# Two of V's 32 key blocks in one group of each layer: from 128 partitions to partitions 0 to 63, in eight-row transfers on ACT's queue

## The chip, the cores and the metric

The kernel runs on one core of one Trainium2 chip. The metric is the time of one execution on the device in microseconds; the figure used is the median of three runs. TensorE, VectorE, ScalarE, GpSimd and SyncE are called PE, DVE, ACT, POOL and SP, as in the profile. The core's transfers run on 16 DMA engines; a transfer is issued by an instruction on SP or on ACT.

## The reference, cut to what matters

Two layers, each a one-token attention step over a cached K and V and then an MLP, in float32:

```python
def _A_ref(x, k_cache, v_cache, wq, wo):
    q = (x @ wq).reshape(B, Sq, H, Dh)            # 32 heads of 128
    scores = einsum("bhqd,bhkd->bhqk", q, k_cache) * Dh ** -0.5
    p = softmax(scores)                           # over 4096 keys
    o = einsum("bhqk,bhkd->bhqd", p, v_cache)
    return o.reshape(B, Sq, H * Dh) @ wo
def _B_ref(x, w1, b1, w2, b2):
    return gelu(layernorm(x) @ w1 + b1) @ w2 + b2
...
x = x + _A_ref(_layernorm(x), k_cache, v_cache, wq, wo)
x = x + _B_ref(_layernorm(x), w1, b1, w2, b2)
```

The last two lines run twice with the same weights and the same K and V, so K and V (67 MB each) are read nearly whole in both layers.

## The kernel before, in words

The 32 heads are taken in eight groups of four (`G`, `J`). Layer 0 runs the groups 0 to 7, layer 1 runs them 7 to 0; `n` counts the groups inside a layer. The host has laid K, V and the weights out so that a group's K is one array of 128 rows by 16384 floats, its V another one. Eight chunks (`C`) of 2048 columns (`NC`) make up such an array; a chunk of V holds four blocks of 128 keys for the four heads (`U` = 512 columns each), so a group's V has 32 blocks. A key's row lies on the partition that is its number modulo 128.

For one group the program does this. `stream` (L356) issues one SP transfer of 128 rows of 64 KB for K through `load` (L83, the issue itself at L85). `scores` (L211) multiplies each chunk by the query, into the PSUM tile `pS`. `softmax` (L216) takes the maximum on DVE, the exponential on ACT (L223), and four PE transposes (L225), so that the weights lie with keys on partitions (`pt`, written by DVE at L227). `stream` issues V in the same way, and `values` (L238) multiplies each chunk by its weights, four matmuls of 512 columns per chunk into `pO` (L241). `scaled_out` (L244) turns the result, `head_out` (L264) multiplies it by the group's Wo (L269), and `queries` (L201) makes the next group's query (L203 to L208). The next group's Wo and Wq are one SP transfer.

All loaded data lives in one large tile, `arena`, which holds three group arrays of 64 KB a partition in turn and some space behind them (`HELD`, `PAIR`). A transfer is issued when its place is free, that is when PE or DVE has read what lay there. SP's order is the order of the calls of `load`. There are 78 transfers from memory on SP, all of 128 rows, and none on another engine. Every transfer also takes one of eight completion counters in turn and waits until the transfer that had it before has landed.

The last group of a layer and the MLP load in smaller pieces. In layer 0 the MLP's matmuls L295 (w1) and L343 (w2) follow the last attention pieces, and the first transfers of layer 1 are issued as these matmuls free their places. The kernel ends with L343 of layer 1, an addition on DVE (L527) and a store of 4 rows (L528). `idle` (L367, the matmul at L368) issues matmuls whose result nobody reads; six stand behind the first group's scores in layer 0.

PE's instructions are themselves fetched from memory while the program runs. The profile lists these fetches as queues of the kind "instruction" (q8 and q14), beside q1, which carries SP's transfers.

Of the kernel before, what the change touches and what calls it, by code (L numbers as in the profile page):

```python
# [17 lines left out]
P = 128  # L18
# [3 lines left out]
G = 8  # L22
J = 4
C = 8
# [3 lines left out]
U = 512  # L28
KEPT = 6

NC = 4 * U
BLOCK = 8 * NC
# [3 lines left out]
HELD = SPARE + 2 * NC  # L36
# [14 lines left out]
FILL = 3  # L51
LAST = ((0, 4), (4, 6), (6, 7))
LAST_IDLE = {3: 1, 5: 1, 6: 1}
WHOLE, HALVES = ((0, 8),), ((0, 4), (4, 8))
VAR_AT = 1


@with_exitstack
def decode_layers(ctx: ExitStack, tc: tile.TileContext, k, v, w, w1, w2, out):
    nc = tc.nc  # L60
# [20 lines left out]
    arena = const.tile([P, ARENA], F32, name="arena")  # L81

    def load(at, src):  # L83
        t = arena[:, at : at + src.shape[-1]]
        tc.keep_in_program_order(nc.sync.dma_start(t, src))  # L85
        return t
# [41 lines left out]
    row, _ = wq_at(0)  # L128
# [3 lines left out]
    ident = ctile("ident", P)  # L132
# [7 lines left out]
    pS, pO, pB = (psum.tile([P, 512], F32, name=n) for n in ("pS", "pO", "pB"))  # L140
# [75 lines left out]
    def softmax(sc, nsc, p):  # L216
        nc.vector.tensor_reduce(mx[:, 0:1], pS, axis=AX.X, op=ALU.max)  # L217
        mt, m, bias = small("mt", 32), small("m"), small("lr", 32)
        nc.vector.transpose(mt, mx)
        nc.vector.tensor_reduce(m, mt[:, :C], axis=AX.X, op=ALU.max)  # L220
        nc.vector.tensor_scalar(mb[:, :C], m.to_broadcast([P, C]), nsc, None, op0=ALU.mult)
        nc.vector.transpose(bias, mb)  # L222
        nc.scalar.activation(p, pS, AF.Exp, bias=bias[:, 0:1], scale=sc, accum_out=mx[:, 0:1])  # L223
        for b in range(4):
            nc.tensor.transpose(pT[:, b].rearrange("p j r -> p (j r)"), p[:, P * b : P * (b + 1)], ident)  # L225
        pt = work.tile([P, J, C, 4], F32, name="pt")
        nc.vector.tensor_copy(pt, pT[:, :, :, :C].rearrange("p b j c -> p j c b"))  # L227
        lt, l, lr, rl = small("mt", 32), small("l"), small("lr", 32), small("rl")
        nc.vector.transpose(lt, mx)  # L229
        nc.vector.tensor_reduce(l, lt[:, :C], axis=AX.X, op=ALU.add)  # L230
        nc.vector.tensor_copy(lt, l.to_broadcast([P, 32]))
        nc.vector.transpose(lr, lt)
        nc.vector.reciprocal(rl, lr[:, 0:1])
        return pt, rl

    def by_head(vt):
        return vt.rearrange("p b (j d) -> p j b d", j=J)

    def values(i, pt, vt, c, of=C):
        for j in range(J):  # L240
            nc.tensor.matmul(pO[32 * j : 32 * j + 4, :], pt[:, j, c, :], by_head(vt)[:, j],  # L241
                             start=(i == 0), stop=(i == of - 1))

    def scaled_out(rl, ot):  # L244
        nc.vector.transpose(ot[:, :512], pO)  # L245
        diag = ot.rearrange("p (b q) -> p b q", q=129)[:, :, :P]
        diag = diag.rearrange("p b (d q) -> p d b q", q=32)[:, :, :, 0]
        o, on = small("o", 4), small("on", 4)
        nc.vector.tensor_reduce(o, diag, axis=AX.X, op=ALU.add)
        nc.vector.tensor_scalar(on, o, rl, None, op0=ALU.mult)  # L250
        return on
# [104 lines left out]
    def stream(what, g, pieces, base):  # L356

        for a, b in pieces:
            t = load(base + NC * a, part(k if what == "k" else v, g, a, b))
            for c in range(a, b):  # L360
                here[what, g, c] = chunk(t, c - a)
                yield c, here[what, g, c]
# [7 lines left out]
    for layer in range(2):  # L370
        order = list(range(G)) if layer == 0 else list(range(G))[::-1]
# [21 lines left out]
        for n, g in enumerate(order):  # L393
# [6 lines left out]
            if layer == 1 and n == 0:  # L400
                tiles = [(c, here["k", g, c]) for c in range(C)]
            elif layer == 1 and n == 1:
                tiles = [(c, here["k", g, c]) for c in range(2)]
                tiles += list(stream("k", g, ((2, 4), (4, 8)), -2 * NC))
                n_kept = STAY + U * KEPT
                load(V1_HOME[6] + n_kept % NC, v[g][:, n_kept:BLOCK])
                for u in range(STAY, n_kept - U, U):
                    nc.scalar.copy(v_next(u), pK[(u - STAY) // U])
                for c in range(STAY // NC, C):
                    here["v", g, c] = chunk(arena[:, V1_HOME[c] : V1_HOME[c] + NC])  # L410
            elif layer == 1 and n == 2:
                tiles = [(c, here["k", g, c]) for c in range(6)]
                tiles += list(stream("k", g, ((6, 8),), 2 * BLOCK - 6 * NC))
            else:
                tiles = stream("k", g, HALVES if first or final else WHOLE, k_home)
            for c, t in tiles:
                scores(z, c, t)
            if first or final:
                for _ in range(FILL if final or layer == 1 else 2 * FILL):
                    idle(t, pO)  # L420
            p, ot = free_now(layer, n)
            if layer == 1 and first:
                z = queries(n + 1, xc_l, wq_next, pO)
                nc.scalar.copy(v_next(STAY + U * KEPT - U), pB)
            pt, rl = softmax(sc, nsc, p)
            if final:
                nc.scalar.activation(small("m"), rl, AF.Gelu_apprx_tanh)

            if layer == 1 and n == 0:
                for c in range(C):  # L430
                    values(c, pt, here["v", g, c], c)
            elif layer == 1 and n == 1:
                for c in range(C):
                    values(c, pt, here["v", g, c], c)

                for pieces, base in ((((0, 4),), K2_HOME), (((4, 6),), SPARE - 4 * NC)):
                    for _ in stream("k", order[2], pieces, base):
                        pass
            elif final:
                last_v = chunk(arena[:, v_home + BLOCK - NC : v_home + BLOCK])  # L440
                for _ in range(FILL - 1):
                    idle(t, pS)
                for c, t in stream("v", g, LAST, v_home):
                    values(c, pt, t, c, C - 1)
                    if c == C - 2:
                        others = scaled_out(rl, ot)
                    for _ in range(LAST_IDLE.get(c, 0)):
                        idle(t, pS)
                for a in (BLOCK - NC, BLOCK - NC // 2):
                    load(v_home + a, v[g][:, a : a + NC // 2])  # L450
                for c in range(C):
                    here["v", g, c] = chunk(arena[:, v_home + NC * c : v_home + NC * (c + 1)])
            else:
                for c, t in stream("v", g, WHOLE, v_home):
                    for i in range(KEPT - 1):
                        if layer == 0 and n == G - 2 and c == (STAY + U * i) // NC:
                            nc.scalar.copy(pK[i], t[:, STAY // U % J + i - J * (c - STAY // NC), :])
                    values(c, pt, t, c)

            if layer == 1 and n == 0:  # L460
                wo_t = chunk(arena[:, PAIR : PAIR + NC])
# [113 lines left out]
```

## Time and profile before

| what | value |
|---|---|
| median of 3 runs | 677.62 us (677.26 to 677.77) |
| the profiled execution's own time | 677.63 us |
| its span, first to last instruction | 675.9 us |
| busy share of PE, DVE, ACT | 60%, 17%, 4% |
| mean granted TensorE clock | 0.806 |
| mean DMA rate over the span | 422 GB/s |

The span leaves out 1.7 us that lie around it. The profile names DMA queues, and gives each packet's time and size, but not which of the 16 engines carried it. A share of 16 engines' time in a stretch is the sum of the times of the packets that start in it, so a short stretch with long packets can show more than 100%.

### The profile page before, as it was taken

How to read it: one execution, taken by the hardware profiler on the slowest of the kernel's cores; microseconds unless marked ns; L12 is line 12 of the kernel's file. 1: busy time of each engine (PE TensorE's matmuls, PEld its weight loads, DVE VectorE, ACT ScalarE, POOL GpSimd, SP SyncE). 2: the span in 40 equal slices, each digit the busy share in tenths (PEclk: the TensorE clock that was granted, in tenths of full speed). 3: DMA queues.
4: the chain of work that ended last, by engine and by line, in shares of the span. 5: the costliest groups of instructions: out<-in, count | busy, mean ns of one | idle time of the engine just before them, and what ended most of it. 6: DMA issues, size and time to landing. Idle time of an engine off the chain costs nothing.

```text
span 675.9 us, 6740 instructions
## 1 busy us (share of the span) xinstructions
PE 408.1 (60%) x3008; PEld 109.8 (16%) x3008; DVE 115.2 (17%) x369; ACT 27.4 (4%) x57; POOL 5.0 (1%) x24
## 2 busy tenths in 40 slices
PE   2745664565534854467597986674466545755596
PEld 1111111111111111111124321111111111111123
DVE  3002110120021201212022322120121111200212
ACT  0010000000000000001011200000000000000010
POOL 1000000000000000000000000000000000000000
PEclk9779776797678865878899998976797767976899
DMA  9999999999999999999999999999999999999995
GB/s 374 435 434 434 435 435 434 413 457 432 428 427 422 444 434 432 434 432 417 433 410 353 427 418 462 407 447 435 426 432 431 432 434 409 461 432 411 426 414 234
DMA packets 11268, 285.34 MB, mean 422 GB/s; under 512 B 1252, under 2 KB 1256, under 8 KB 3688
## 3 DMA queue, kind: packets, MB, share of 16 engines
q1 hardware_dynamic: 11240, 284.92, 98.6%
q8 instruction: 23, 0.38, 0.2%
q14 instruction: 5, 0.04, 0.0%
HBM read 284.92 MB, written 0.00 MB: 422 GB/s over the span
## 4 chain that ended last, share of the span: by engine, by line
PE 40%; DMA 39%; another core or an unknown queue 14%; DVE 4%; ACT 1%; issue 1%; ACTq 0%; SPq 0%; DVEq 0%
DMA arena<-in_v 35%; PE pO L241 19%; PE pS L213 12%; DMA arena<-in_w 4%; PE pB L269 4%; PE pO L207 1%; PE pO L225 1%; ACT arena L223 1%; PE pS L368 1%; DVE arena L245 1%; DVE smalls L217 1%; PE pO L368 0%; PE pO L343 0%; DVE arena L205 0%
## 5 line engine op out<-in xcount | busy, mean ns | idle before, releaser
L213 PE MATMUL pS<-arena,smalls 128*8 128x512 f32 x1024 | 148.3, 732 | 112.5 <-DMA arena<-in_k 111.6
L241 PE MATMUL pO<-arena,pt 128*4 128x512 f32 x1008 | 139.9, 700 | 79.1 <-DMA arena<-in_v 78.6
L269 PE MATMUL pB<-arena,smalls 128*1 128x512 f32 x112 | 52.8, 616 | 21.9 <-DVE smalls L250 15.9
L213 PEld LDWEIGHTS pS<-arena,smalls 128*8 128x8 f32 x1024 | 30.1, 103 | 214.9 <-issue 190.9
L241 PEld LDWEIGHTS pO<-arena,pt 128*4 128x4 f32 x1008 | 28.4, 95 | 178.0 <-issue 175.2
L217 DVE TENSOR_REDUCE smalls<-pS 128x1 f32<-128x512 f32 x16 | 11.1, 692 | 253.1 <-PE pS L213 253.1
L245 DVE STREAM_TRANSPOSE arena<-pO 128x512 f32<-128x512 f32 x16 | 11.5, 717 | 217.1 <-PE pO L241 217.1
L223 ACT ACTIVATE arena<-pS,smalls 128x512 f32<-128x512 f32 x16 | 12.4, 778 | 536.2 <-DVE smalls L222 536.2
L205 DVE SCALAR_TENSOR_TENSOR arena<-arena,smalls 128x512 f32<-128x512 f32 x45 | 33.8, 752 | 1.6
L225 PE MATMUL pO<-ident,arena 128*128 128x128 f32 x64 | 13.2, 341 | 33.8 <-ACT arena L223 33.5
L269 PEld LDWEIGHTS pB<-arena,smalls 128*1 128x1 f32 x112 | 8.6, 85 | 65.9 <-issue 38.2
L207 PE MATMUL pO<-smalls,arena 128*128 128x1 f32 x120 | 16.6, 259 | 3.3 <-DVE arena L205 3.3
L207 PEld LDWEIGHTS pO<-smalls,arena 128*128 128x128 f32 x120 | 15.3, 200 | 15.5 <-DVE arena L205 13.8
L225 PEld LDWEIGHTS pO<-ident,arena 128*128 128x128 f32 x64 | 8.5, 169 | 47.7 <-ACT arena L223 46.5
L368 PE MATMUL pO<-arena,ident 128*8 128x512 f32 (+1 forms) x38 | 15.9, 547 | 0.0
L368 PE MATMUL pS<-arena,ident 128*8 128x512 f32 (+1 forms) x34 | 14.0, 517 | 0.5 <-DVE pt L307 0.5
L203 DVE TENSOR_SCALAR arena<-arena,smalls 128x512 f32<-128x512 f32 x15 | 7.2, 480 | 4.7 <-DMA arena<-in_w 4.7
L343 PE MATMUL pO<-arena,smalls 128*1 128x128 f32 x176 | 5.9, 272 | 3.3 <-DMA arena<-in_w 2.2
L208 DVE COPY smalls<-pO 128x4 f32<-128x4 f32 x15 | 2.5, 165 | 26.5 <-PE pO L207 26.5
L169 PE MATMUL pO<-smalls 128*32 128x1 f32 x64 | 2.0, 184 | 7.4 <-DVE smalls L163 6.3
L229 DVE STREAM_TRANSPOSE smalls<-smalls 128x32 f32<-128x32 f32 x16 | 3.4, 211 | 17.5 <-ACT arena L223 17.5
L295 PE MATMUL pS<-arena,smalls 128*2 128x128 f32 (+1 forms) x160 | 4.9, 259 | 1.9 <-DMA arena<-in_w 1.9
(92 smaller groups left out, 101.2 us busy)
## 6 DMA issues: line engine op xcount, KB each, us to landing
arena<-in_k SPq DMA_DIRECT2D x8, 4096.0 KB, 26.0
arena<-in_w SPq DMA_DIRECT2D x13, 2048.0 KB, 33.2
arena<-in_v SPq DMA_DIRECT2D x2, 4096.0 KB, 38.4
arena<-in_k SPq DMA_DIRECT2D x3, 2048.0 KB, 15.9
arena<-in_v SPq DMA_DIRECT2D x2, 2048.0 KB, 41.6
arena<-in_w SPq DMA_DIRECT2D x4, 1024.0 KB, 16.3
arena<-in_w SPq DMA_DIRECT2D x6, 512.0 KB, 13.3
arena<-in_v SPq DMA_DIRECT2D x2, 1024.0 KB, 43.2
```

Of the source, the lines that this page charges most:

```text
L203: pin(nc.vector.tensor_scalar(t, wt[:, 0, :], xc[:, 0:1], None, op0=ALU.mult))
L205: nc.vector.scalar_tensor_tensor(t, wt[:, c, :], xc[:, c : c + 1], t, op0=ALU.mult, op1=ALU.add)
L207: nc.tensor.matmul(at[:, j : j + 1], t[:, P * j : P * (j + 1)], one, start=True, stop=True)
L213: nc.tensor.matmul(pS[32 * j : 32 * j + C, :], z[:, j, C - 1 - c : 2 * C - 1 - c], kt[:, j, :], start=(c == 0), stop=(c == C - 1))
L217: nc.vector.tensor_reduce(mx[:, 0:1], pS, axis=AX.X, op=ALU.max)
L223: nc.scalar.activation(p, pS, AF.Exp, bias=bias[:, 0:1], scale=sc, accum_out=mx[:, 0:1])
L225: nc.tensor.transpose(pT[:, b].rearrange("p j r -> p (j r)"), p[:, P * b : P * (b + 1)], ident)
L241: nc.tensor.matmul(pO[32 * j : 32 * j + 4, :], pt[:, j, c, :], by_head(vt)[:, j], start=(i == 0), stop=(i == of - 1))
L245: nc.vector.transpose(ot[:, :512], pO)
L269: nc.tensor.matmul(pB[0:1, :], on[:, d : d + 1], wt[:, d, :], start=n == 0 and d == 0, stop=n == G - 2 and d == 3)
L343: pin(nc.tensor.matmul(pM[32 * j : 32 * j + 1, :], g[:, c - b0 : c - b0 + 1], w2_t[c][:, P * j : P * (j + 1)], start=(c == 0), stop=(c == ...
L368: pin(nc.tensor.matmul(at[:C, :n], ident[:, :C], t[:, 0, :n], start=True, stop=True))
```

## The change

In one group of each layer (`MOVED_OF`: group n = 4 in layer 0, n = 5 in layer 1) the last two blocks of V's 32, 1024 columns, are no longer part of the 128-row V transfer, which is 15360 columns there. The host copies the half of these blocks that lay on partitions 64 to 127 into unused columns behind rows 0 to 63 of the array, so that each of the rows 0 to 63 holds 2048 contiguous columns, 8 KB: its own half and that of row 64 higher. `load_moved` brings them in with eight transfers of eight rows each (row numbers first, first + 4, ... first + 28), issued on ACT's queue: three, three and two of them in the three groups ahead of the one that uses them. The same bytes are read in all.

In that group `second_half` makes two more PE transposes and a DVE copy, to bring the weights of keys 64 to 127 to partitions 0 to 63, and the last chunk's four matmuls of 512 columns become twelve of 256 columns (`values_in_halves`). Also, the six idle matmuls of the first group in layer 0 go.

```diff
+LOWER, MOVED = P // 2, 2
+MOVED_OF = 4, 5
+MOVED_ROWS = {1: (0, 3), 2: (3, 6), 3: (6, 8)}, {2: (0, 3), 3: (3, 6), 4: (6, 8)}
+MOVED_AT = 3 * BLOCK, 2 * BLOCK + 2 * NC
+HALF_AT = HELD + 2 * NC + U + 4 * 129, 2 * BLOCK + 3 * NC
...
+    def load_moved(layer, g, parts):
+        t = arena[:LOWER, MOVED_AT[layer] : MOVED_AT[layer] + 2 * MOVED * U]
+        for q in range(*parts):
+            first = q % 4 + 32 * (q // 4)
+            rows = slice(first, first + 29, 4)
+            nc.scalar.dma_start(t[rows], v[g][rows, BLOCK - MOVED * U : BLOCK + MOVED * U])
+        return t.rearrange("p (h b j d) -> h p j b d", h=2, b=MOVED, j=J)
+
+    def second_half(layer, p):
+        for i in range(MOVED):
+            b = 4 - MOVED + i
+            nc.tensor.transpose(pO[:LOWER, P * i : P * (i + 1)], p[:, P * b + LOWER : P * (b + 1)], ident)
+        t = arena[:LOWER, HALF_AT[layer] : HALF_AT[layer] + J * MOVED].rearrange("p (j b) -> p j b", j=J)
+        nc.vector.tensor_copy(t, pO[:LOWER, : P * MOVED].rearrange("p (b j r) -> p j b r", b=MOVED, j=J)[:, :, :, C - 1])
+        return t
+
+    def values_in_halves(pt, pt_half, vt, moved):
+        b = 4 - MOVED
+        for j in range(J):
+            at = pO[32 * j : 32 * j + 4]
+            nc.tensor.matmul(at[:MOVED, : P * MOVED], pt_half[:, j], moved[1][:, j], start=False, stop=False)
+            nc.tensor.matmul(at[:, P * b :], pt[:LOWER, j, C - 1, :], moved[0][:, j], start=False, stop=False)
+            nc.tensor.matmul(at[:, : P * b], pt[:, j, C - 1, :], by_head(vt)[:, j, :b], start=False, stop=True)
...
+            halved = n == MOVED_OF[layer]
+            if n in MOVED_ROWS[layer]:
+                moved = load_moved(layer, order[MOVED_OF[layer]], MOVED_ROWS[layer][n])
             for c, t in tiles:
                 scores(z, c, t)
             if first or final:
-                for _ in range(FILL if final or layer == 1 else 2 * FILL):
+                for _ in range(FILL if final or layer == 1 else 0):
                     idle(t, pO)
...
             pt, rl = softmax(sc, nsc, p)
+            if halved:
+                pt_half = second_half(layer, p)
...
-                for c, t in stream("v", g, WHOLE, v_home):
+                if halved:
+                    t = load(v_home, v[g][:, : BLOCK - MOVED * U])
...
-                    values(c, pt, t, c)
+                    if halved and c == C - 1:
+                        values_in_halves(pt, pt_half, t, moved)
+                    else:
+                        values(c, pt, t, c)
...
+    for g in (MOVED_OF[0], G - 1 - MOVED_OF[1]):
+        arrays["v"][g, :LOWER, BLOCK : BLOCK + MOVED * U] = arrays["v"][g, LOWER:, BLOCK - MOVED * U : BLOCK]
```

ACT's instructions at the start of layer 0, of the kernel before (`pK` are PSUM tiles that keep a part of V for layer 1):

```order
L223 ACT_TABLE_LOAD
L223 ACTIVATE arena,smalls<-pS,smalls 128x512 x7
L457 COPY pK_78<-arena 128x512
L457 COPY pK_79<-arena 128x512
L457 COPY pK_80<-arena 128x512
```

The same place of the changed kernel, whose line 228 is line 223 of the kernel before:

```order
L228 ACT_TABLE_LOAD
L228 ACTIVATE arena,smalls<-pS,smalls 128x512
L255 DMA arena<-in_v 8x2048 x3
L228 ACTIVATE arena,smalls<-pS,smalls 128x512
L255 DMA arena<-in_v 8x2048 x3
L228 ACTIVATE arena,smalls<-pS,smalls 128x512
L255 DMA arena<-in_v 8x2048 x2
L228 ACTIVATE arena,smalls<-pS,smalls 128x512 x4
```

The eight new transfers stand between the exponentials of the first four groups, each lot behind one exponential and ahead of the next.

PE's instructions of group n = 4 in layer 0, of the kernel before, from its scores to the next group's query:

```order
L213 MATMUL pS<-arena,smalls 8x512 x32
L225 MATMUL pO<-ident,arena 128x128 x4
L241 MATMUL pO<-arena,pt 4x512 x32
L269 MATMUL pB<-arena,smalls 1x512 x4
L207 MATMUL pO<-smalls,arena 128x1 x4
```

The same group of the changed kernel (the triple of rows for the first head is followed by three more like it, then by L301 and L212, which are L269 and L207 of the kernel before):

```order
L218 MATMUL pS<-arena,smalls 8x512 x32
L230 MATMUL pO<-ident,arena 128x128 x4
L262 MATMUL pO<-ident,arena 64x128 x2
L246 MATMUL pO<-arena,pt 4x512 x28
L272 MATMUL pO<-arena 2x256
L273 MATMUL pO<-arena,pt 4x256
L274 MATMUL pO<-arena,pt 4x256
```

Two transposes and eight matmuls have come to this group, and four of the 512-column matmuls have become twelve of half the width.

## Rows read from the trace of the kernel before

**Rows 1.** The page: DMA share in 40 slices; queues with packets, MB, share of 16 engines.
```profile
DMA  9999999999999999999999999999999999999995
...
q1 hardware_dynamic: 11240, 284.92, 98.6%
q8 instruction: 23, 0.38, 0.2%
```

**Rows 2.** Chain that ended last, at both layers' ends: start us, us, what.
```profile
353.52 11.31 DMA arena<-in_w
364.87 0.83 PE pS L295 x32
...
658.91 13.33 DMA arena<-in_w
672.28 0.66 PE pO L343 x16
```

**Rows 3.** DMA queues of the stretch 31 to 33 us: packets, MB, share.
```profile
q1 hardware_dynamic: 16, 1.05, 122.4%
q8 instruction: 1, 0.02, 3.3%
```

**Rows 4.** DMA queues of 32.6 to 32.8 us: the packet behind that fetch.
```profile
q1 hardware_dynamic: 1, 0.07, 91.0%
```

**Rows 5.** DMA queues of 84.5 to 86 us, then of 85.2 to 85.3 us.
```profile
q14 instruction: 1, 0.01, 1.4%
...
q1 hardware_dynamic: 1, 0.07, 192.5%
```

**Rows 6.** DMA queues of 0 to 364 us, then of 370 to 668 us.
```profile
q8 instruction: 10, 0.16, 0.2%
...
q8 instruction: 11, 0.18, 0.2%
q14 instruction: 3, 0.02, 0.0%
```

**Rows 7.** A stretch at layer 0's end: us, busy (x) by engine, PEclk, DMA share, GB/s.
```profile
364.00:364.50 0.50, 0.50 (x14) 0.17 (x2) 0.00 (x0) 0.00 (x0) 0.00 (x0) 1.00 0.57 203
```

**Rows 8.** The same view, stretches at the end of the kernel.
```profile
668.50:669.00 0.50, 0.00 (x0) 0.00 (x0) 0.46 (x2) 0.08 (x1) 0.00 (x0) 1.00 0.49 176
669.00:669.50 0.50, 0.28 (x12) 0.29 (x16) 0.00 (x0) 0.20 (x1) 0.00 (x0) 1.00 0.16 66
...
670.00:670.50 0.50, 0.50 (x28) 0.41 (x16) 0.00 (x0) 0.00 (x0) 0.00 (x0) 1.00 0.10 41
670.50:671.00 0.50, 0.22 (x8) 0.00 (x0) 0.00 (x0) 0.00 (x0) 0.00 (x0) 1.00 0.06 25
...
671.50:672.00 0.50, 0.37 (x16) 0.07 (x4) 0.00 (x0) 0.00 (x0) 0.00 (x0) 1.00 0.02 8
```

**Rows 9.** DMA queues of 356.9 to 357.4 us, a stretch of 8 KB rows.
```profile
DMA packets 29, 0.18 MB, mean 361 GB/s; under 512 B 7, under 2 KB 7, under 8 KB 7
...
q1 hardware_dynamic: 29, 0.18, 87.0%
```

**Rows 10.** PE in order of time, around groups n = 4 (layer 0) and 5 (layer 1).
```profile
220.50 9.54 PE L241 MATMUL pO<-arena,pt 128*4 128x512 f32 x64 [6.97 <-DMA arena<-in_v]
...
244.76 1.90 PE L213 MATMUL pS<-arena,smalls 128*8 128x512 f32 x8 [8.82 <-DMA arena<-in_k]
573.72 8.72 PE L241 MATMUL pO<-arena,pt 128*4 128x512 f32 x64 [5.63 <-DMA arena<-in_v]
```

**Rows 11.** Groups of instructions, shapes apart: busy us, mean ns, idle before.
```profile
L225 PE MATMUL pO<-ident,arena 128*128 128x128 f32 x64 | 13.2, 341 | 33.8 <-ACT arena L223 33.5 <-DVE smalls L231 0.3
L368 PE MATMUL pS<-arena,ident 128*8 128x256 f32 x12 | 3.1, 379 | 0.5 <-DVE pt L307 0.5
```

**Rows 12.** ACT and SP's issues in order of time.
```profile
125.60 0.78 ACT L223 ACTIVATE arena<-pS,smalls 128x512 f32<-128x512 f32 x1 [43.13 <-DVE smalls L222]
...
166.13 0.33 SPq L85 DMA_DIRECT2D arena<-in_v  x1
```

More of the change, by code (lines that the diff above doesn't have):

```diff
@@ L453, in decode_layers @@
             else:
-                for c, t in stream("v", g, WHOLE, v_home):
+                if halved:
+                    t = load(v_home, v[g][:, : BLOCK - MOVED * U])
+                    pieces = [(c, arena[:, v_home + NC * c : v_home + NC * (c + 1)]) for c in range(C)]
+                    pieces = [(c, t.rearrange("p (b n) -> p b n", n=U)) for c, t in pieces]
+                for c, t in pieces if halved else stream("v", g, WHOLE, v_home):
                     for i in range(KEPT - 1):
```

## The prediction, made before the changed kernel ran

> **What bounds the kernel now.** I read the page first: the DMA share is 9 tenths or more in every slice but the last, and q1, the loads, takes 98.6% of 16 engines' span [rows 1]. The kernel is bound by its transfers, so PE, DVE and ACT count only where they hold a transfer up. The chain of waits then tells which transfers: at the end of layer 0 it waits 11.31 us for w and goes on with L295 at 364.87, and at the end of the kernel it waits 13.33 us for w and closes with L343 at 672.28 [rows 2]. A wait for a transfer ends when the slowest of the 16 engines has landed its part. So I looked at how evenly the engines finish, which the page doesn't show.
>
> Short stretches show it. Near the end of layer 0, from 364.0 to 364.5, the share is 0.57, nine engines of 16 [rows 7]: the other seven have run out of work. At the end of the kernel the share is 0.49 at 668.5, 0.16 at 669.0, 0.10 at 670.0, then 0.06, one engine of 16, from 670.5 on, and 0.02 after 671.5, where the last packet ends at about 671.8 [rows 8]. One engine alone keeps the kernel from ending for 1.3 us, and two more are over half a microsecond behind the rest, which is through by about 669.2.
>
> **Why engines fall behind** is in the instruction queues. Between 31 and 33 us one packet of q8 takes 3.3% of 16 times 2 us, 1.06 us [rows 3]. The 64 KB packet behind it on the same engine takes 91.0% of 16 times 0.2 us, 2.91 us [rows 4]; the other 15 of that stretch take (122.4% of 32 us less 2.91) / 15 = 2.42 us [rows 3]. So a fetch sets its engine back by 1.06 + 0.49 = 1.55 us. A fetch of q14, half the size, takes 1.4% of 24 us, 0.34, and the packet behind it 192.5% of 1.6 us, 3.08: 0.34 + 0.66 = 1.00 us [rows 5]. Following packets from one's end to the next one's start, I find the q8 fetches going to eight engines in turn, and the q14 ones to the other eight. The nine engines still at work in rows 7 agree: eight with q8 fetches and one with a q14 fetch. Up to 364 us there are ten fetches of q8, so two of the eight have had two; from 370 to 668 there are eleven, so three have had two [rows 6], and three late engines are what rows 8 show. No row says which partitions these eight serve. That is the first unknown.
>
> **The change part by part.** In each layer, rows 64 to 127 lose 4 KB each and rows 0 to 63 get 4 KB more each: 8 KB in a packet of their own, less 4 KB in the long one. I read the row lists (first, first + 4, to first + 28) as one row for each of eight engines, the same eight each time, those that serve the lower rows. In a sentence by itself: the Trainium skill (DMA: Bandwidth & Descriptors, "The descriptor swizzle") states such a map, engines 0 to 7 for partitions 0 to 63; no run here shows it.
>
> - Upper engines, eight rows each: 4 KB is a sixteenth of 2.42 us, 0.15 us, so 8 x 0.15 = 1.21 us less per layer.
> - Lower engines: an 8 KB row costs (87.0% of 8 us less seven four-byte signals) / 22 = about 0.31 us, and its signal 0.01 [rows 9]. Eight of them, 2.57 us, less 1.21 saved in the long transfer: 1.36 us more per layer.
> - A second queue. Each eight-row transfer makes its engine turn from SP's queue to ACT's and back, which the kernel before never does for loads. Bounds: rows 9 hold seven changes of transfer inside SP's queue at no price, so 0; and a fetch costs beyond its bytes 1.55 - 0.63 = 0.92 (q8) or 1.00 - 0.31 = 0.69 us (q14) [rows 3 to 5, 9]. Less than nothing is excluded, since an extra packet frees no engine. I take 0, because these are rows from memory to the arena, queued well ahead like those of rows 9, and not code that an engine has just asked for. The Trainium skill (the same page, "Issuing engines are not separate DMA queues") says that transfers of several issuers interleave on the same engines, and names no price for the turn; by it the sum would stay as it is.
> - Layer 0's end: the two engines with two fetches stand 2 x 1.55 = 3.10 us back. If they are upper ones they now stand 1.89 back; a lower one with the q14 fetch stands 1.00 + 1.36 = 2.36 and is late next. Gain: 3.10 - 2.36 = 0.74 us. It passes on whole, since L295 and L343 wait for the last engine there, and layer 1's first transfers wait for these matmuls.
> - The kernel's end: the last engine goes from 671.8 to 670.6. The lower ones, through by 669.2, end at 670.56, just beneath it. Gain: 1.21 us.
> - PE and DVE: per layer two more transposes of some 0.34 us, a small DVE copy, and eight more matmuls of at most 0.38 us [rows 11], together under 4.5 us. The transposes fall into the wait for V (6.97 and 5.63 us), the matmuls ahead of a wait for K of 8.82 us in layer 0 [rows 10]; with that cover gone they would cost these 4.5 us. SP's next transfers are queued more than a group ahead. The six idle matmuls stood ahead of such a wait too; going without them costs nothing.
> - ACT: eight issues of some 0.33 us, as on SP, beside 43 us of idle time between exponentials [rows 12]. Behind the waiting issue stands the next exponential. What the issues wait for (a place read long before, a counter whose last transfer landed a group earlier) is there when ACT comes to them, so 0.
> - The fetches come where PE has worked off some 260 more instructions; 28 more in all (matmul and weight load counted) shift them by less than a group of matmuls, so each engine keeps its number of fetches.
>
> The sum is 0.74 + 1.21 = 1.95 us. The profiled execution took 677.63 us, 0.01 from the median, so **675.7 us**.
>
> **The rivals.**
>
> *Each turn to ACT's queue costs like a fetch.* Place: lower engines, eight turns per layer. At 0.69 us each, they stand 1.36 + 5.5 = 6.9 us back. Layer 0: 1.00 + 6.9 = 7.9 against 3.10, 4.8 us lost; layer 1: 669.2 + 6.9 = 676.1 against 671.8, 4.3 lost; 686.7 us. If the three transfers of a group go in one turn, it is 2.1 us in place of 5.5: 1.4 and 0.9 lost, 679.9 us. With eight turns at s each the sum is 1.95 - 16 s, so it decides at s = 0.12 us. For it: every turn to another queue in this trace has cost over 0.6 us. Against it: these were all fetches of code.
>
> *The eight late engines serve the lower rows*, so the change loads the wrong half: 1.36 us lost at each end, 680.3 us. Nothing in the rows speaks against it.
>
> *It moves nothing that counts.* If an eight-row transfer is spread over all 16 engines, each loses and gets the same: 677.6 us. The Trainium skill's table in the same page ("Rules for kernel authors") says of transfers to partition halves not to bother, since both halves spray across all engines; its section on the number of engines gives eight rows eight engines. No run here shows either. The same time comes out where a turn costs between 0.04 and 0.2 us: the gain shrinks to under 1.3 us or to nothing, 676.3 to 679.0 us.
>
> **How the numbers follow.** 0.2%, 1.4 us, is about what a measurement of this kernel can tell from no change. The forecast has 0.48: its terms rest on rows, its two unknowns (which half, what a turn costs) don't. Its own range is 674.4 to 676.2, the lower end for a last engine that gets fewer late packets than here. No change that can be told has 0.20. Slower has 0.32: 0.20 for dear turns, 0.12 for the wrong half. The range, 674.4 to 681.5, takes in the forecast, no change, the wrong half and turns shared by a group; it leaves out the eight dear turns and a larger gain.
>
> **What would show it.** Right: a second queue of 128 packets of 8 KB with their signals; between 364 and 365 more engines at work than nine, L295 about 0.7 us earlier; at the end no engine alone for over half a microsecond, and L343's last wait some 1.9 us earlier. Dear turns: long packets over 2.42 us behind each 8 KB packet around 36, 82 and 126 us. The wrong half: the single late engine alone for longer than 1.3 us. It would be wrong altogether if PE's or ACT's waits in the middle of a layer grew, so that the DMA share fell below 9 tenths there.

## The result: a little slower, 1.0017 times the kernel before

The changed kernel took 678.99 us in the median of 19 runs, the kernel before 677.79 us in 19 runs beside it. The ratio is 1.0017 (1.0009 to 1.0025), 1.2 us. The forecast was 675.7 us; 678.99 lies inside the range, and the sign was wrong. The profiled execution took 679.19 us, with a span of 677.4 us (675.9 before).

The second queue is there as described. These are the queues of the page of the changed kernel, which answer to [rows 1]:

```profile
q1 hardware_dynamic: 11240, 283.88, 98.0%
q10 hardware_dynamic: 256, 1.05, 0.4%
q8 instruction: 24, 0.39, 0.2%
```

The 256 packets are 128 rows of 8 KB and their 128 signals. The kernel is still bound by its transfers. The end of the kernel, the view of [rows 8] at the changed kernel:

```profile
668.50:669.00 0.50, 0.40 (x24) 0.12 (x16) 0.32 (x4) 0.00 (x0) 0.00 (x0) 1.00 0.88 356
...
670.00:670.50 0.50, 0.50 (x32) 0.49 (x25) 0.39 (x2) 0.00 (x0) 0.32 (x3) 1.00 0.32 131
...
671.50:672.00 0.50, 0.50 (x28) 0.47 (x24) 0.42 (x2) 0.06 (x2) 0.00 (x0) 1.00 0.13 53
672.00:672.50 0.50, 0.37 (x16) 0.07 (x4) 0.00 (x0) 0.19 (x1) 0.00 (x0) 1.00 0.12 49
672.50:673.00 0.50, 0.42 (x16) 0.40 (x20) 0.00 (x0) 0.00 (x0) 0.00 (x0) 1.00 0.14 57
```

The reader should see the next-to-last column, the DMA share: from 671.5 to 673.0 it stays at 0.12 to 0.14, two engines of 16. Before, one engine was left for 1.3 us; now two are left for about 2 us, and the last one ends 1.6 us later. The chain that ended last says the same:

```profile
589.30 29.49 DMA arena<-in_v
...
661.86 11.94 DMA arena<-in_w
673.85 0.66 PE pO L375 x16
```

The last w lands at 673.80 us (661.86 + 11.94); in [rows 2] it was 658.91 + 13.33 = 672.24. The staircase in which the engines end one after another, and which the change was to cut, has grown.

Something else has changed, at the border of the layers. PE's granted clock there, stretches of 2 us, first in the kernel before, then in the changed one (columns as in [rows 7]; the third number from the end is the clock):

```profile
360.00:362.00 2.00, 1.05 (x32) 0.77 (x32) 0.32 (x2) 0.21 (x1) 0.00 (x0) 1.00 0.99 409
362.00:364.00 2.00, 0.77 (x29) 0.76 (x33) 0.63 (x3) 0.21 (x1) 0.19 (x1) 1.00 0.97 400
364.00:366.00 2.00, 1.49 (x46) 0.74 (x34) 0.21 (x1) 0.00 (x0) 0.10 (x1) 1.00 0.81 222
366.00:368.00 2.00, 1.87 (x27) 1.01 (x31) 0.53 (x3) 1.35 (x2) 0.19 (x1) 1.00 0.94 378
```

```profile
360.00:362.00 2.00, 1.32 (x28) 0.95 (x32) 0.13 (x1) 0.21 (x1) 0.00 (x0) 0.66 1.03 416
362.00:364.00 2.00, 1.27 (x28) 0.61 (x24) 0.77 (x3) 0.21 (x1) 0.19 (x1) 0.50 0.92 381
364.00:366.00 2.00, 2.00 (x40) 1.07 (x33) 0.00 (x0) 0.00 (x0) 0.00 (x0) 0.50 0.69 222
366.00:368.00 2.00, 1.50 (x29) 0.91 (x21) 0.58 (x3) 0.00 (x0) 0.29 (x2) 0.63 0.87 310
```

In the changed kernel the clock is 0.50, 1.2 GHz, from some 360.7 to 367.5 us; before it is 1.00, 2.4 GHz, all along. What that does stands in the order of time, first of the kernel before, then of the changed one (start us, us, what; L375 is L343, L563 is L519 before: DVE's first transpose of layer 1):

```profile
363.23 1.05 PE L343 MATMUL pO<-arena,smalls 128*1 128x128 f32 x32 [1.44 <-DMA arena<-in_w]
364.87 0.79 PE L295 MATMUL pS<-arena,smalls 128*2 128x88 f32 x32 [0.17 <-DMA arena<-in_w]
...
370.32 0.32 DVE L519 STREAM_TRANSPOSE pt<-pO 128x128 f32<-128x128 f32 x1 [3.72 <-PE pO L343]
```

```profile
360.68 1.88 PE L327 MATMUL pS<-arena,smalls 128*2 128x128 f32 x32 [1.53 <-DMA arena<-in_w]
...
363.29 1.89 PE L375 MATMUL pO<-arena,smalls 128*1 128x128 f32 x32 [0.73 <-DMA arena<-in_w]
364.96 0.51 PE L327 MATMUL pS<-arena,smalls 128*2 128x88 f32 x6
365.81 1.38 PE L327 MATMUL pS<-arena,smalls 128*2 128x88 f32 x26
...
371.69 0.32 DVE L563 STREAM_TRANSPOSE pt<-pO 128x128 f32<-128x128 f32 x1 [3.54 <-PE pO L375]
```

The w at 364.87 lands at the same time in both (364.82 and 364.88 us for the part that comes last), so the predicted 0.74 us of layer 0 is not there. On top of it PE is not ready: L375 takes 1.89 in place of 1.05 us, idle matmuls stretch too, the last w1 group ends at 367.19 in place of 365.66, and layer 1 begins 371.69 - 370.32 = 1.37 us late.

So two readings were open. **Balance:** the engines that are late are not all relieved. **Clock:** TensorE's lower clock at the border costs the time. In the expectations below theory A is the balance and theory B the clock. Theory C is, for e3 and e4, that the second queue itself costs the time; from e9 on, that balance and clock are two terms that add up.

### The profile page after: what moved, and what is told of

Same layout as the page of the kernel before. It is cut to its first block, busy times and chain, and to the rows that moved or that the text cites. A ratio compares the mean times of both kernels' runs of the same rounds, so it can differ in the third digit from the quotient of the medians.

```text
span 677.4 us, 6832 instructions
## 1 busy us (share of the span) xinstructions
PE 409.8 (61%) x3032; PEld 110.8 (16%) x3032; DVE 115.0 (17%) x371; ACT 27.3 (4%) x57; POOL 5.0 (1%) x24
## 3 DMA queue, kind: packets, MB, share of 16 engines
q10 hardware_dynamic: 256, 1.05, 0.4%
## 5 line engine op out<-in xcount | busy, mean ns | idle before, releaser
L218 PE MATMUL pS<-arena,smalls 128*8 128x512 f32 x1024 | 141.1, 700 | 106.3 <-DMA arena<-in_k 105.4
L246 PE MATMUL pO<-arena,pt 128*4 128x512 f32 x992 | 138.5, 713 | 82.9 <-DMA arena<-in_v 82.5
L301 PE MATMUL pB<-arena,smalls 128*1 128x512 f32 x112 | 51.9, 607 | 20.8 <-DVE smalls L282 15.8
L230 PE MATMUL pO<-ident,arena 128*128 128x128 f32 x64 | 11.8, 313 | 38.0 <-ACT arena L228 37.6
L301 PEld LDWEIGHTS pB<-arena,smalls 128*1 128x1 f32 x112 | 8.5, 84 | 63.1 <-issue 36.3
L212 PE MATMUL pO<-smalls,arena 128*128 128x1 f32 x120 | 16.6, 259 | 3.3 <-DVE arena L210 3.3
L212 PEld LDWEIGHTS pO<-smalls,arena 128*128 128x128 f32 x120 | 15.3, 200 | 15.5 <-DVE arena L210 13.8
L400 PE MATMUL pO<-arena,ident 128*8 128x512 f32 (+1 forms) x26 | 10.6, 526 | 0.0
L375 PE MATMUL pO<-arena,smalls 128*1 128x128 f32 x176 | 7.5, 298 | 1.4 <-DMA arena<-in_w 1.4
L327 PE MATMUL pS<-arena,smalls 128*2 128x128 f32 (+1 forms) x160 | 6.9, 307 | 1.7 <-DMA arena<-in_w 1.7
```

The costliest lines, as they stand in the source:

```text
L212: nc.tensor.matmul(at[:, j : j + 1], t[:, P * j : P * (j + 1)], one, start=True, stop=True)
L218: nc.tensor.matmul(pS[32 * j : 32 * j + C, :], z[:, j, C - 1 - c : 2 * C - 1 - c], kt[:, j, :], start=(c == 0), stop=(c == C - 1))
L301: nc.tensor.matmul(pB[0:1, :], on[:, d : d + 1], wt[:, d, :], start=n == 0 and d == 0, stop=n == G - 2 and d == 3)
L375: pin(nc.tensor.matmul(pM[32 * j : 32 * j + 1, :], g[:, c - b0 : c - b0 + 1], w2_t[c][:, P * j : P * (j + 1)], start=(c == 0), stop=(c == ...
L400: pin(nc.tensor.matmul(at[:C, :n], ident[:, :C], t[:, 0, :n], start=True, stop=True))
```

## The experiments

The trace also tells when each of a transfer's 16 parts landed. "Lag" below is how far the last engine is behind the first one, at layer 0's last w (it lands at 366 to 368 us) and among the last w transfers of the kernel; it is read in one profiled execution each, while the ratio is over all runs. Single executions differ: the one profiled of e9 took 680.03 us, 1.75 us more than the median of e9.

| run | ratio to before (95%) | lowest clock, 360 to 368 us | DVE's first transpose of layer 1 | lag, layer 0 and kernel's end |
|---|---|---|---|---|
| before | 1 | 1.00 | 370.32 | 3.16, 4.93 |
| changed | 1.0017 (1.0009 to 1.0025) | 0.50 | 371.69 | 4.32, 5.55 |
| changed again (e14) | 1.0024 (1.0014 to 1.0034) | 0.50 | 372.43 | 4.41, 6.03 |
| five idles (e9) | 1.0011 (1.0002 to 1.0020) | 1.00 | 370.36 | 4.47, 5.49 |
| five idles again (e15) | 1.0010 (1.0001 to 1.0018) | 1.00 | 370.44 | 4.35, 5.87 |
| layer 1 alone (e12) | 1.0011 (1.0000 to 1.0023) | 1.00 | 370.20 | 3.24, 4.49 |
| relief alone (e10) | 0.9984 (0.9975 to 0.9992) | 0.50 | 370.17 | 3.20, 4.83 |
| four rows (e11) | 1.0017 (1.0008 to 1.0026) | 0.50 | 372.53 | 4.53, 3.65 |
| four rows, five idles (e13) | 1.0000 (0.9991 to 1.0009) | 1.00 | 370.99 | 4.49, 3.62 |

**The idle matmuls and the move apart.** e1 is the kernel before without the six idle matmuls, e2 the changed kernel with them:

```diff
e1 (kernel before)
-                for _ in range(FILL if final or layer == 1 else 2 * FILL):
+                for _ in range(FILL if final or layer == 1 else 0):
e2 (changed kernel)
-                for _ in range(FILL if final or layer == 1 else 0):
+                for _ in range(FILL if final or layer == 1 else 2 * FILL):
```

> The kernel before, without the six idle matmuls alone. Theory A (balance of the 16 DMA engines: PE's code fetches go to eight engines in turn, six of which the change relieves by 1.21 us and two of which it loads by 1.36 us per layer): the matmuls carry no load of an engine, so the time of before, ratio 1.000 within 0.001. Theory B (the loss sits in PE at the layers' border, where the granted clock was 0.50 in the changed kernel's profile and 1.00 in that of before, because the idle matmuls are gone): the change's ratio, 1.0017, and again 0.50 between 361 and 367 us.

> The change with the six idle matmuls kept. Theory A: the ratio of the change, 1.001 to 1.0025. Theory B: 1.000, and a clock of 1.00 at the border.

Measured: e1 678.18 us, 1.0007 (0.9998 to 1.0016); e2 679.12 us, 1.0027 (1.0018 to 1.0037). The loss is the move's. What the idle matmuls cost or gain can't be told from nothing. The clock was 1.00 at the border in e1 and 0.50 in e2, so theory B's reason for it, the missing idle matmuls, is out.

**The second queue with another shape.** e3 brings the same bytes in eight transfers of 16 rows by 4 KB, meant to leave the balance as it was; e4 mirrors the change to rows 64 to 127.

```diff
e3
-            first = q % 4 + 32 * (q // 4)
-            rows = slice(first, first + 29, 4)
-            nc.scalar.dma_start(t[rows], v[g][rows, BLOCK - MOVED * U : BLOCK + MOVED * U])
+            rows, a = slice(q % 4, q % 4 + 61, 4), MOVED * U * (q // 4)
+            nc.scalar.dma_start(t[rows, a : a + MOVED * U], v[g][rows, BLOCK - MOVED * U + a : BLOCK + a])
e4
-            first = q % 4 + 32 * (q // 4)
+            first = LOWER + q % 4 + 32 * (q // 4)
...
```

> The change with the same rows and bytes, in eight transfers of 16 rows by 1024 columns in place of 8 rows by 2048. Theory A: 16 rows go over all 16 engines, each gets back what the shorter V transfer took from it, and the time is that of before, 1.000 within 0.001; the last engine of the kernel stands 3 to 5 us behind the first, as before. Theory C (the second queue, ACT's issues or the extra PE and DVE work cost the time, whatever engine carries the rows): 1.0017 or more.

> The change mirrored: the two blocks' keys on partitions 64 to 127, in eight-row transfers into these partitions. Theory A with engines bound to partitions: six of the eight engines with PE's fetches get 1.36 us more per layer, 3.10 + 1.36 us behind at both ends, 2.7 us lost, ratio 1.004. Theory A with engines taken by the shape of a transfer (eight rows, always the same eight engines): the time of the change, 1.0017, and the same engines late. Theory C: 1.0017.

Measured: e3 684.32 us, 1.0093 (1.0080 to 1.0106); e4 686.67 us, 1.0133 (1.0120 to 1.0146). Both are far dearer than the change; e4 missed every expectation (1.004 at most), and e3 missed what it was made for. The rows on ACT's queue themselves are slower in e4. DMA queues of a stretch with eight such rows, of the changed kernel (68.5 to 68.9 us), then of e4 (69.0 to 69.4 us):

```profile
DMA packets 26, 0.20 MB, mean 492 GB/s; under 512 B 16, under 2 KB 16, under 8 KB 16
...
q10 hardware_dynamic: 16, 0.07, 40.3%
```

```profile
DMA packets 22, 0.20 MB, mean 492 GB/s; under 512 B 12, under 2 KB 12, under 8 KB 12
...
q10 hardware_dynamic: 14, 0.07, 45.8%
```

A share of 16 engines and 0.4 us is a share of 6.4 us: eight rows took 2.58 us with their signals in the changed kernel, 0.32 each, and 2.93 us in e4, 0.37 each. Over all 128 rows the trace has a mean of 312 ns against 357 (up to 532). By following packets, the eight rows go to the two engines with fetches of 1026 ns and to six without a q8 fetch in e4 too, as in the changed kernel: a transfer of eight rows keeps to the same eight engines wherever its rows lie. That it is dearer in e4 because the long transfers reach those partitions through the other eight is an inference; no run took it apart further. As controls of the turn's price e3 and e4 are of no use. The price shows in the changed kernel itself: 0.32 us a row with its signal, what [rows 9] gave without any turn.

**The clock, first attempt.** e5 and e6 put nine idle matmuls into the waits for w at the border, in the changed kernel and in the one before. They write into `pS`, over sums of layer 0's hidden layer, so its MLP is not computed in these two.

```diff
         ht = turned(0)
+        if fill is not None:
+            for _ in range(5):
+                idle(fill, pS, 2 * P)
         hidden(1 if fill is not None else 2)
+        if fill is not None:
+            for _ in range(4):
+                idle(fill, pS, 2 * P)
```

> The changed kernel with nine more idle matmuls at the end of layer 0: five of 256 columns behind the first w1 group of matmuls (L327) and four behind the second, all of them in waits for w of 1.5 us each. In the profile of the changed kernel TensorE's granted clock falls from 1.00 to 0.50 at about 360.7 us and the two groups behind it take 1.88 and 1.89 us in place of 1.05; layer 1's first k landing ends 1.8 us later than before although the last w of layer 0 lands at the same time (367.4 against 367.3). Theory A (the engines' balance alone: which engines take q8's fetches): these matmuls change nothing, 679.0 us, 0.2% above before. Theory B (the lost clock at the border is the larger part of the loss): the granted clock stays at 1.00 from 360 to 367 us, L327 and L375 take 1.05 us again, and the time is 1.2 to 1.8 us below the changed kernel's, 677.2 to 677.8 us, the same as before or up to 0.1% under it.

> The kernel before with the same nine idle matmuls at the end of layer 0. Its granted clock is 1.00 there already. Theory A and theory B both: no change, 677.5 us within 0.1%. If the idle matmuls themselves cost something (they delay a group whose w has landed), it shows here alone, as up to 0.5 us.

Measured: e5 678.99 us, 1.0022 (1.0014 to 1.0031); e6 677.89 us, 1.0003 (0.9992 to 1.0015). The clock stayed at 1.00 in e5 and the time did not move. That spoke against the clock, but the four late idle matmuls delayed the group behind them to 363.75 us in place of 363.29, and layer 1 still began at 370.76 us, so that a third of the 1.37 us stayed. e6 makes that a weak excuse: there the same nine begin layer 1 at 371.13 us, 0.81 us late, and the time is that of before. So e5 stands against the clock, and a late border isn't passed on whole to the end. It was done again with five idle matmuls (e9).

**One layer at a time.** e7 has the change in layer 0 alone, e8 and e12 in layer 1 alone (one kernel twice; the trace that is read is e12's).

```diff
e7
-MOVED_OF = 4, 5
+MOVED_OF = 4, G
...
e8, e12
-MOVED_OF = 4, 5
+MOVED_OF = G, 5
...
```

> The change in layer 0 alone; layer 1 loads V as before. Theory A (balance): in the slot counting of the traces the last engine of layer 0 gains 0.2 us for five of the eight places at which the round of fetches can start and loses 1.4 for three, on average a loss of 0.4 us: 678.0 us (1.0006). Theory B (lost clock): the fall of the clock comes with layer 0's move, so the whole loss of the changed kernel is here: 678.8 to 679.5 us (1.0017 to 1.0027), with a granted clock of 0.50 to 0.66 from 361 to 367 us.

> The change in layer 1 alone; layer 0 loads V as before (its six idle matmuls at the start stay out). Theory A (balance): the last engine of the kernel gains 0.2 us in half of the runs and loses 1.4 in the others, on average a loss of 0.6 us: 678.2 us (1.0009). Theory B (lost clock): the clock at the border stays at 1.00 and what is left is the balance of layer 1, between a gain of 0.2 and a loss of 0.6 us: 677.4 to 678.2 us. The two agree here if the balance is as counted; a time above 678.6 speaks against B.

> The change in layer 1 alone once more, for its trace. All theories: about 678.4 us as in the run of it before. Granted clock 1.00 from 352 to 370 us. Theory A: at the last w the engine that is last behind the first one lags by 4.1 us if the two lower engines with fetches have one each (1.55 + 1.36 + 1.21), and by 5.7 us if one of them has two, as in the changed kernel (5.57). A lag of under 3.5 us speaks against it.

Measured: e7 678.40 us, 1.0008 (0.9999 to 1.0017), with the clock at 0.50 from 361 to 367 us; e8 678.55 us, 1.0011 (1.0001 to 1.0020); e12 678.53 us, 1.0011 (1.0000 to 1.0023), clock 1.00 throughout. By the ratios layer 1 loses 0.75 us with no help from the clock, layer 0 about 0.5 us; together 1.25, the change's loss. e7 lies between the times of the two theories (678.0 us, and 678.8 or more). Each of the two is near the edge of what can be told: the intervals of e7 and e12 reach down to nothing. The lag at e12's end, 4.5 us, fits one fetch each on the loaded engines (4.1 expected) better than two (5.7).

**The clock, second attempt.** e9 and e15 are one kernel: the five early idle matmuls alone, into `pO`, where they harm nothing. e14 is the changed kernel beside e15 on one chip.

```diff
         ht = turned(0)
+        if fill is not None:
+            for _ in range(5):
+                idle(fill, pO, 2 * P)
```

> The changed kernel with five idle matmuls of 256 columns behind the first w1 group of layer 0's end alone, where TensorE waits 1.5 us for w; the four that stood behind the second group in the run before, and delayed the group after it by 0.46 us, are left out. The granted clock should stay at 1.00 from 360 to 367 us, and the first transpose of layer 1 (DVE, 128x128 from pO) should start at 370.3 us as before in place of 371.7. Theory A (balance alone counts): no change against the changed kernel, 679.0 us. Theory C (the loss is the clock at the border plus the balance of layer 1): 1.4 us less, 677.6 us, the time of before.

> The changed kernel once more, on the same chip as the run below. All theories: 679.0 us (1.0017); granted clock 0.50 to 0.66 from 361 to 367 us.

> The changed kernel with the five idle matmuls once more. Theory C: 0.5 to 1.4 us below the run above, 677.6 to 678.5 us. Theory A alone: the same time as the run above.

Measured: e9 678.28 us, e15 678.31 us, e14 679.39 us; ratios in the table. In order of time, e9 at the border:

```profile
363.27 1.05 PE L378 MATMUL pO<-arena,smalls 128*1 128x128 f32 x32 [1.54 <-DMA arena<-in_w]
364.90 0.79 PE L327 MATMUL pS<-arena,smalls 128*2 128x88 f32 x32 [0.17 <-DMA arena<-in_w]
...
370.36 0.32 DVE L566 STREAM_TRANSPOSE pt<-pO 128x128 f32<-128x128 f32 x1 [3.73 <-PE pO L378]
```

The border is as it was before the change, to 0.04 us, and the kernel is still 1.0011 times before (e15: 1.0010); both intervals leave out 1. So about 0.1%, 0.7 us, is lost with the clock at 1.00, which leaves the balance. By the trace of e9, layer 0's move then costs nothing and gains nothing, and the 0.7 us are layer 1's, the loss that e8 and e12 show alone. What the clock is worth is less firm. On one chip e15 is 1.08 us faster than e14, the changed kernel, but their intervals overlap; e9 is only 0.0006 below the changed kernel, less than the noise; and e5, with the clock at 1.00, gained nothing. A clock term of about 0.1% is likely, not shown.

**Relief without load.** e10 fetches only the 4 KB of rows 0 to 63 that are their own; the keys of rows 64 to 127 in two blocks are left out of the sum of values.

```diff
-            nc.scalar.dma_start(t[rows], v[g][rows, BLOCK - MOVED * U : BLOCK + MOVED * U])
+            nc.scalar.dma_start(t[rows, : MOVED * U], v[g][rows, BLOCK - MOVED * U : BLOCK])
...
-            nc.tensor.matmul(at[:MOVED, : P * MOVED], pt_half[:, j], moved[1][:, j], start=False, stop=False)
```

> The change without its load: the eight-row transfers bring the 4 KB of rows 0 to 63 that are their own, and the 4 KB of rows 64 to 127 are not fetched at all, so those keys of two blocks are left out of the sum of values. Upper engines are relieved by 1.21 us as in the changed kernel, lower ones stand where they stood (eight rows of 4 KB, some 0.16 us each, against 1.21 us less in the long transfer). Theory A (two of the eight engines that fetch PE's code are lower ones, and their load ate the gain): the last engine gains 1.2 us in each layer whenever the engines with two fetches are upper ones, five starts of eight in layer 0 and four of eight in layer 1: on average 1.3 us less than before, 676.4 us, or up to 677.8 if the clock at the border falls here too. Rival (the engines that are late are not the relieved ones at all): no gain, 677.8 us with the clock at 1.00 and 679.0 us without.

Measured: 676.65 us, 0.9984 (0.9975 to 0.9992), 1.15 us faster than before, where 1.3 on average was expected. The end of its chain, which answers to [rows 2]:

```profile
659.45 11.93 DMA arena<-in_w
...
671.43 0.66 PE pO L374 x16
```

The last w lands at 671.39 us in place of 672.24. The staircase is about as long as before (lag 4.83 against 4.93); it is the whole of it that ends earlier. At layer 0's end the relief is there as foretold, and the clock hides it: the last w lands at 366.13 us in place of 367.32, 1.19 us earlier, but the clock is at 0.50 from 361.8 to 365.2 us, L374 (L375 in the changed kernel) takes 1.89 us again, and layer 1 begins at 370.17 us, only 0.15 us earlier than before.

It also loads 0.5 MB less, but from upper rows only, which is the relief itself; lower engines carry what they carried. So relieving the upper engines does gain, and what loses is the load on the lower ones: from 0.9984 to 1.0017, over 2 us. Some of that can be the border's, since the clock was low for 3.4 us in e10 and for 6.8 us in the changed kernel.

**Load on four engines that carry no fetch.** e11 sends the moved bytes in transfers of four rows, e13 adds the five idle matmuls. Traffic alone: V's last block is not read from where it lands, so it is missing from the values.

```diff
-            rows = slice(first, first + 29, 4)
+            rows = slice(first, first + 13, 4)
...
-                    t = load(v_home, v[g][:, : BLOCK - MOVED * U])
+                    t = load(v_home, v[g][:, : BLOCK - MOVED * U // 2])
...
```

> Traffic alone, V's last block is not read from where it lands, so the sum of values is left wrong by that block: the long V transfer is 2 KB a row shorter on all 128 rows, and eight transfers of four rows of 8 KB (rows 0 to 15 and 32 to 47) carry the same number of bytes on ACT's queue. If four rows go to four engines, these get 8 x 0.31 - 0.6 = 1.9 us more and the other twelve 0.6 us less. Theory A: where the two lower engines that fetch PE's code are not among the four, the engines with two fetches gain 0.6 us in each layer, 1.2 us in all: 676.6 us, plus up to 1.4 if the clock at the border falls. Where they are among the four, these stand 1.55 + 1.9 = 3.5 us back, or 5.0 with two fetches: 678.0 to 681.0 us. The trace shows which: the fetches that last 1018 ns are those of the two lower engines.

> The four-row traffic of the run before (V's last block still not read from where it lands, so the values are left wrong by that block) with the five idle matmuls that kept the clock. In the run before, the four loaded engines carried no fetch of PE's code, the engine that was last at the kernel's end lagged by 3.65 us in place of 4.93, but the granted clock fell at the border and layer 1 began 2.1 us late, for 679.4 us. Theory C (balance and clock are two separate terms): the clock stays at 1.00, the border falls back to before's time, and the gain at the end stays: 676.4 to 677.2 us. Theory A alone (the clock does not count): 679.4 us again, and then the loss of the four-row version has another cause.

Measured: e11 679.38 us, 1.0017; e13 677.94 us, 1.0000 (0.9991 to 1.0009). By following packets, the 64 rows of q10 land on four engines, and in layer 0 none of these four carries a fetch of q8; at a landing near 223 us three of the four stand 2.5 to 2.7 us behind the first engine, as worked out (1.9 + 0.6), and the fourth, which had a fetch of q14, 3.6 us. The lag at the end falls to 3.6 us from 4.93, the one place where the gain is seen. It is not seen in the time: e11 loses at the border (clock 0.50, 2.2 us late), and in e13, where the clock stays up, a fetch of q14 at 360.4 us falls on the engine that was last anyway (3.5 us of lag become 4.5), and layer 1 begins 0.67 us late. With the idle matmuls the four-row version is 0.17% faster, which speaks for clock and balance as two terms, as theory C has it; but the 676.4 to 677.2 us of theory C were missed, and no version tried that computes the whole reference beats the kernel before.

## Why the prediction was wrong, step by step

- **The bound** (transfers; the slowest engine sets both ends) was right for the kernel's end. At the border the transfers set it alone only while PE's clock is up.
- **A turn to a second queue, s = 0**, was right: 0.32 us a row, and near 222 us the six engines of the loaded half without a fetch stand 2.51 to 2.80 us behind the first one, where 1.36 + 1.21 = 2.57 puts them without a price for the turn. So the dear turns, the rival with 0.20, did not come. Nor did "it moves nothing": transfers of eight rows went to eight engines. The Trainium skill (DMA: Bandwidth & Descriptors, "Why a DMA increments its semaphore by 16 and not by 1") states that a transfer gets the largest number of engines, up to 16, that divides its rows; by that, four rows go to four engines, and e11's trace agrees. The advice cited in the prediction, not to bother, speaks of halves spread over all engines; eight-row transfers are not spread so.
- **The sizes of relief and load** were right. At that landing the first engine is 1.14 us earlier than before (1.21 foretold), and three of the four loaded engines of e11 stood where the price of an 8 KB row puts them.
- **The failed step: "If they are upper ones".** The eight engines with q8 fetches were taken as one half. They are six of the relieved half and two of the loaded half. Following packets in the changed kernel, the fetches at 189.3 and 227.0 us fall on two engines that each carry eight rows of q10; the six others carry none. In layer 0 such an engine stands 1.55 + 1.36 = 2.91 us back, and the 3.10 of before becomes 2.91, not 2.36: 0.2 us left of 0.74. To an engine relieved by 1.21 that is a lag of 4.12. Near 222 us the engine with the fetch of 189.3 is the last and lags 4.18 us, where 1.76 was the largest lag before; at layer 0's last w the two lag 4.10 and 4.19. At the kernel's end the two have two fetches each, 3.10 + 1.36 + 1.21 = 5.67, seen 5.57 and 5.28. In layer 1 this count is weaker than in layer 0: in the kernel before it gives 3.10 where 4.93 is seen, since three engines stand 1.7 to 2.2 us back already at 376 us, and no run tells why.

The stretch of 189.0 to 189.5 us in the changed kernel has the first of these two fetches, 12.7% of 16 times 0.5 us, 1.02 us:

```profile
q8 instruction: 1, 0.02, 12.7%
```

- **"Each engine keeps its number of fetches"** failed for q14 at the border. Up to 363.5 us the kernel before has one q14 fetch, the changed kernel two: the second comes at 360.8 us in place of 363.8. It falls on an engine that was 3.35 us behind and makes it the last, at 4.32, so that even the 0.2 us of layer 0 are not seen.
- **Who has two fetches is not fixed.** The prediction counted as if the round always started at one engine. Between 30 and 340 us the q8 fetches of the two engines in the loaded half last 1016 to 1026 ns, those of the six others 1055 to 1108, which tells them apart, and the traces start the round at different engines: so which ones are hit twice differs from run to run. Counted over the eight possible starts, the change gains 0.2 us or loses 1.4 in each layer, by the start; the mean is a loss of some 1 us for both, an estimate that takes each start as equally likely.
- **PE's additions are hidden:** this was right for the matmuls. The twelve narrower ones run from 583.4 to 589.3 us in layer 1, 5.9 us where four of before took about 1.1 (an eighth of 8.72, [rows 10]): 4.8 us, a little above the bound of 4.5. The V transfer that waits for them is issued 6.8 us later than before (589.30 against 582.51) but lands only 1.6 us later (618.79 against 617.21), about as late as layer 1 began, so they are covered. **A term was missing:** PE's clock at the border. It was 1.00 there before, and the prediction took PE's pace for granted. What it costs lies between nothing (e5) and some 1.1 us (e14 against e15, e11 against e13).

The same V transfer in the chain of the kernel before:

```profile
582.51 34.70 DMA arena<-in_v
```

- **The rival "wrong half"** (680.3 us) had the right mechanism for two of the eight engines, and the right sign.

The cause of the clock's fall stays open. It fell at the border in all eight profiles without added idle matmuls in which layer 0's move was made in some form (the changed kernel, e2, e3, e4, e7, e10, e11, e14), and in none of the three without it (before, e1, e12). Yet the waits ahead of it are the same, 1.54 and 1.53 us before the second w1 group, and PE's busy time from 352 to 360 us is 5.77 us before, 5.34 in e1, 5.34 in the changed kernel and 5.76 in e14.

## What to carry to other kernels

When the slowest DMA engine sets the end, list per engine what it carries, background fetches included, before shifting bytes from one group of engines to another: a group that is late on average may have members in the half that is to be loaded, and one of them is enough. Test the relief and the load in separate runs; here they were worth 1.15 us and over 2 us of opposite sign, and the sum told neither; what the clock took stands in both. Look at the granted clock at every border where PE waits for transfers; five idle matmuls in a wait kept it up, and the time was then lower by 0.06 to 0.17% in three comparisons; nine kept it up too, and the time was no lower.

## What the runs showed that was not expected

- An eight-row transfer to partitions 64 to 127 takes the same eight engines as one to partitions 0 to 63, and its 8 KB rows take 357 ns on average, up to 532, in place of 312 (e4). With 16 rows of 4 KB on partitions 0 to 63 every engine stood some 1.95 us later by 225 us, though all carried the same bytes as before (e3).
- The round in which the fetches go to eight engines starts at different engines in different executions of one program. In the two profiles of the changed kernel the fetches of 1016 to 1018 ns are the fifth and sixth of the kernel in one and the sixth and seventh in the other (e14). The time of the kernel before scatters from 676.2 to 680.8 us over all its runs; that the start of the round is the reason was not tested.
